# One table of steps for all engines, from batch 1 on, in an attention and Mish kernel

## The chip, the cores and the metric

The kernel runs on one core of one Trainium2 chip. The metric is the device time of one execution in microseconds, as the median of the runs shown; lower is better.

## The reference

Eight batches, each with 8 heads of 512 tokens and 32 states of width 64. First, tokens read from states and states read from tokens, by a softmax each; then both kinds of rows (544 per batch, 512 wide) go through two dense layers with a Mish-like function between them.

```python
scores = scale * (x @ state.T)
xread = softmax(scores) @ state
sread = softmax(scores.T) @ x
rows = concatenate([xread, sread])
h = rows @ w_in
out = (h * tanh(softplus(h))) @ w_out
```

Everything is float32. The kernel reaches that accuracy by splitting each operand into a high part and a low part (in the code h and l: gh and gl, ah and al, swh and swl), and by three matmuls for each product: high by high, low by high, high by low.

## The kernel before

The token rows of a batch never stand in memory as such. For each batch the kernel folds the states into the first weights (`sw_slice`, L567: the state weights, in PSUM as swp, split into swh and swl), so that the first products are the attention weights (aT, split into ah and al) times the state weights. The state reads (`sread`, L495, kept in srds) are collected over all batches and go through the layers once, as an item of their own called "s" between batch 6 and batch 7.

A batch has 8 slots of 2 x 128 hidden columns each. In a slot TensorE makes the first products of both column blocks (`gemm1`, L614, into the banks ph), and ScalarE applies Mish. From batch 2 on the result is held as units: a unit is one half p of a batch's tokens in one slot, so 16 per batch, in ten buffers. `prepare` (L1051) splits a unit into gh and gl, and `consume` (L1079) multiplies it by the second weights (wo). The units of slots 0 to 4 (`SEVEN`, L30) go by seven products of 256 columns instead of four of 512: `prepare` makes four sums on GpSimd for it, and `seven_weights` (L891) makes sums of the weights, once per slot index. The units of slots 5 to 7 go directly. The 8 units of one half p form a span with four PSUM banks (one, two, top, end); the sums of the first two are formed behind the fifth unit, and the results are stored behind the last one (`result`, L675). Batch 1 still uses the direct way for all (`gemm2`, L698), two slots behind.

Beside this, each batch prepares the attention of the next: x is turned (`x_transposed`), moved between partitions by DMA (`x_moved`, L294), multiplied by the states (`scores`), and goes through both softmaxes; `e2_turned` (L389) turns the exps of the second one and moves them by 16 DMAs, and `sread` uses them. The state weights of batches from 2 on come from a copy of w_in in DRAM, 1 MB at a time (`load_w_in_again`, L561).

What sets the order: the steps up to batch 0 are a list written out by hand, in which TensorE, GpSimd, VectorE and ScalarE keep to the program's order (class `InOrder`, L60). At L881 that is switched off for VectorE and ScalarE. From there `around` (L928) and `after` (L960) say per slot what is emitted, and the scheduler orders VectorE, ScalarE and the DMA queue of SP by its own estimate, bound only by the marks of `behind` (L257). `two_next` (L1111) prepares two units at the end of a slot. TensorE and GpSimd keep the order of the program. Batch 6 ends with `sreads_moved` (L536, 16 DMAs, its turned copy in the buffer "wt" that also holds a span's sums) and `sreads_split` (L547). `gemm1_s` (L645) is the first layer of the item "s".

```python
    dve.on = act.on = False
...
        if key == B - 2 and j == 6:
            with behind("mish"):
                sreads_moved()
...
        if j == SEVEN - 1:
            e = spans[key, p]["sums"] = pool.tile([P, 4, 256], F32, tag="wt", name=f"sums_{key}_{p}", bufs=1)
```

Of the kernel before, what the change touches and what calls it, by code (L numbers as in the profile page):

```python
# [9 lines left out]
F32 = mybir.dt.float32  # L10
# [19 lines left out]
SEVEN = 5  # L30
G = 4 * P
# [49 lines left out]
def state_attention_mish_kernel(ctx, tc, x, state, w_in, w_out, out):  # L81
# [454 lines left out]
    def sreads_moved():  # L536

        u = pool.tile([P, 4, B - 1, NS], F32, tag="wt", name="sr_turned", bufs=1)
        dve.transpose(
            u.rearrange("p s b n -> p b s n"), srds[0][:, :B - 1].rearrange("p b k (i d) -> p b (k i) d", i=2))  # L540
        srds["moved"] = pool.tile([P, NC, B - 1, NS], F32, tag="sc", name="sr_moved", bufs=1)
        for s in range(4):
            for c in range(NC):
                nc.sync.dma_start(  # L544
                    srds["moved"][quad(s), c].rearrange("p b n -> p (b n)"), u[quad(c), s].rearrange("p b n -> p (b n)"))

    def sreads_split():  # L547
        both = pool.tile([P, NC, 2, B * NS], F32R, tag="raw", name="srT", bufs=2)
        srT.extend(both[:, :, i] for i in range(2))
        srT.append(both)  # L550
        srT_parts(early, srds["moved"].rearrange("p c b n -> p c (b n)"))

    def sread_transposed():
        pt = first_bank("srTp")[:, :P]
        pe.transpose(pt, srds[0][:, B - 1].rearrange("p k d -> p (k d)"), ident)
        srT_parts(range(B - 1, B), pt.rearrange("p (c n) -> p c n", n=NS))
# [88 lines left out]
    def gemm1_s(j, r, w_rows, unit):  # L645

        for k in range(2):
            fc = 2 * r + k
            ph = (first_bank, misc)[k](f"ph_s_{j}_{r}_{k}")
            w = w_rows[:, :, fc * P:(fc + 1) * P]  # L650
            hi, lo = (pool.tile([P, NC, P], F32R, tag="t", name=f"w{n}_{j}_{r}_{k}", bufs=5) for n in "hl")
            act.copy(hi, w)
            dve.tensor_sub(lo, w, as_f32(hi))

            for c in range(NC):
                pe.matmul(
                    ph, hi[:, c], srT[2][:, c].rearrange("p i t -> p (i t)"), start=(c == 0), stop=(c == NC - 1))
            for c in range(NC):
                pe.matmul(
                    ph[:, :256], lo[:, c], srT[0][:, c], start=False, stop=(c == NC - 1), skip_group_check=True)  # L660
            to = unit[:, 1 - k].rearrange("f h t -> f (h t)")
            act.copy(to, ph[:, 256:])
            dve.tensor_add(to, to, ph[:, :256])
            last["mish"] = act.activation(to, to, AF.Mish)

    def store(key, t, o):
        if key == "s":
            for b4 in range(4):
                r0 = (4 * t + b4) * T + S
                nc.sync.dma_start(out[r0:r0 + NS, :], o[b4 * NS:(b4 + 1) * NS, :])  # L670
        else:
            to = out[key * T:key * T + S, :]
            last["store"] = nc.sync.dma_start(to.rearrange("(p t) e -> p t e", t=NT)[:, t], o)

    def result(key, t, acc, sums=None, op=None):  # L675
        if (key, t) == (B - 1, NT - 1):
            last_o = pool.tile([P, DM], F32, tag="e2T", name=f"o_{key}_{t}", bufs=1)
            for i, part in enumerate((slice(0, 256), slice(256, 512))):
                o = last_o[:, part]
                dve.tensor_tensor(o, acc[:, part], sums[:, i], op)  # L680
                (nc.scalar if part.start else nc.sync).dma_start(
                    out[key * T:key * T + S, part].rearrange("(p t) e -> p t e", t=NT)[:, t, :], o)
            return
        o = pool.tile([P, DM], F32, tag="o", name=f"o_{key}_{t}", bufs=2)
        if sums is not None:
            dve.tensor_tensor(*(a.rearrange("t (h e) -> t h e", h=2) for a in (o, acc)), sums, op)
        elif t % 2 == 0:
            dve.tensor_copy(o, acc)
        else:
            act.copy(o, acc)  # L690
        store(key, t, o)
# [6 lines left out]
    def gemm2(key, fcs, gh, gl, ntok, ts=None):  # L698
# [3 lines left out]
        for t in ts or range(ntok):  # L702
# [9 lines left out]
            if fcs[-1] == NFC - 1:  # L712
                result(key, t, accs[key][t])
# [167 lines left out]
    dve.on = act.on = False  # L881

    with behind("load"):
        sn_next = load_state(2)

# [5 lines left out]
    def seven_weights(j):  # L891
# [5 lines left out]
        pool_e.tensor_add(  # L897
# [5 lines left out]
        low, high = (wo[j][:, 0, n, 256:] for n in range(2))  # L903
        act.copy(high, w[:, 0])
        dve.tensor_sub(low, w[:, 0], as_f32(high))
        low, high = (wx[0][:, j, n] for n in range(2))
        act.copy(high, w[:, 1:])
        dve.tensor_sub(low, w[:, 1:], as_f32(high))

    def products(j):  # L910
# [4 lines left out]
        if j < SEVEN:  # L915
# [9 lines left out]
    own = at1  # L925
    spans = {}

    def around(key, j):  # L928


        nonlocal own, prev, sn_next
        more = key + 1 < B
        if j == 0:
            prev = own
            if more:
                own = attention(key + 1, sn_next, x_ins.pop(key + 1))
                aTs[key + 1] = own["aT"]

        beside = []
        if key == 1 and j == 1:  # L940
            beside += [sw_slice(key, 2)]
# [234 lines left out]
```

## Time and profile before

| what | value |
|---|---|
| median of 3 runs | 667.32 us (666.57 to 667.61) |
| profiled execution | 668.79 us, its span 667.0 us |
| mean granted TensorE clock | 0.976 |
| busy: TensorE, VectorE, ScalarE, GpSimd | 637.2, 427.0, 331.2, 165.3 us |
| matmuls | 5108 |

The span runs from the first to the last instruction of the profiled execution. A busy TensorE is not one at its peak: matmuls are pipelined, and the time of one in the tables includes its way through the array. Waits are put down to what ended them.

### The profile page before, as it was taken

The page shows a single profiled execution, that of the slowest core. Times are in us where ns is not written, and L with a number is a line of the kernel's source. Part 1 is how long each engine was busy: PE and PEld are TensorE (multiplying, and loading weights), DVE is VectorE, ACT ScalarE, POOL GpSimd, SP SyncE. Part 2 cuts the span into 40 slices and gives each one's busy share as a digit, 9 for nine tenths or more (in the row PEclk, how much of TensorE's full clock was granted, in tenths as well). Part 3 has the DMA queues.
Part 4 walks back from the last instruction along what each step waited for, and adds up shares of the span by engine and source line. Part 5 has one row for each costly group of instructions (what it writes and reads, how often), then busy time and mean ns, then how long its engine had stood idle before and what let it go on. Part 6 is the DMA issues. An engine that isn't in the chain of part 4 may idle for free.

```text
span 667.0 us, 12927 instructions
## 1 busy us (share of the span) xinstructions
PE 637.2 (96%) x5108; PEld 533.4 (80%) x5108; DVE 427.0 (64%) x731; ACT 331.2 (50%) x654; POOL 165.3 (25%) x226
## 2 busy tenths in 40 slices
PE   8999999997996979999999999999999799999997
PEld 6776778784885769798988898888887589888996
DVE  6998974777328553877378646964594577335353
ACT  5998852543336433745365434734282375434330
POOL 0000030365223110352017300640050052515200
PEclk9999999998996979999999999999999799999999
DMA  8999826412515252633354254425253341301000
GB/s 331 408 337 315 287 73 173 128 32 64 166 62 186 71 163 66 202 116 110 120 194 124 69 162 148 160 73 158 75 172 96 130 159 28 132 1 28 6 32 32
DMA packets 69036, 89.84 MB, mean 135 GB/s; under 512 B 13808, under 2 KB 42224, under 8 KB 68976
## 3 DMA queue, kind: packets, MB, share of 16 engines
q1 hardware_dynamic: 68544, 88.83, 41.4%
q8 instruction: 40, 0.66, 0.4%
q10 hardware_dynamic: 432, 0.20, 0.1%
q14 instruction: 20, 0.16, 0.1%
HBM read 63.90 MB, written 13.11 MB: 115 GB/s over the span
## 4 chain that ended last, share of the span: by engine, by line
PE 75%; DMA 8%; DVE 6%; SPq 3%; POOL 3%; ACT 2%; issue 1%; DVEq 0%; ACTq 0%
PE ph L73 22%; PE acc_top L73 13%; PE acc_end L73 10%; PE acc L73 6%; PE acc_two L73 6%; PE acc_one L73 6%; PE swp L73 4%; DMA wir<-in_moe_w_in_dram 3%; PE ph_s L73 3%; POOL w_sums L73 3%; DMA x<-in_x_dram 2%; DMA wor<-in_moe_w_out_dram 2%; SPq L544 1%; DVE gl L73 1%; PE acc_s_top L73 1%
## 5 line engine op out<-in xcount | busy, mean ns | idle before, releaser
L73 POOL TENSOR_TENSOR sums<-u 128x256 f32<-128x256 f32 x60 | 53.6, 893 | 310.8 <-DVE u L73 81.0
L73 ACT ACTIVATE u<-ph 128x256 f32<-128x256 f32 x192 | 63.0, 384 | 121.6 <-PE ph L73 119.6
L73 DVE TENSOR_TENSOR gl<-u,gh 128x384 fp32r<-128x384 f32 (+1 forms) x96 | 62.7, 653 | 62.6 <-ACT gh L73 59.6
L73 PE MATMUL ph<-ah,swh 128*128 128x512 f32 (+1 forms) x260 | 83.3, 402 | 10.2 <-DVE swl L73 8.7
L73 PE MATMUL acc_top<-wo,gh 128*128 128x256 f32 (+1 forms) x384 | 92.7, 330 | 0.0
L73 PE MATMUL ph<-al,swh 128*128 128x512 f32 (+1 forms) x260 | 81.5, 396 | 0.2 <-DVE al L73 0.2
L73 PE MATMUL ph<-ah,swl 128*128 128x512 f32 (+1 forms) x260 | 81.4, 394 | 0.1
L73 PE MATMUL acc<-wo,gh 128*128 128x512 f32 x256 | 79.9, 393 | 0.0
L73 POOL TENSOR_TENSOR sums<-sums,u 128x128 f32<-128x128 f32 x120 | 70.3, 586 | 9.4
L73 PEld LDWEIGHTS acc_top<-wo,gh 128*128 128x128 f32 x384 | 64.7, 194 | 8.8 <-DVE srds L73 1.6
L73 ACT CAST gh<-u 128x384 fp32r<-128x384 f32 x60 | 30.9, 515 | 70.2 <-PE acc_end L73 61.3
L73 PEld LDWEIGHTS ph<-ah,swh 128*128 128x128 f32 x260 | 47.7, 194 | 22.3 <-DVE swl L73 9.6
L73 PE MATMUL acc_top<-wo,gl 128*128 128x256 f32 (+1 forms) x192 | 62.7, 326 | 0.0
L73 PEld LDWEIGHTS ph<-al,swh 128*128 128x128 f32 x260 | 49.9, 193 | 11.3 <-DVE al L73 0.4
L73 PEld LDWEIGHTS ph<-ah,swl 128*128 128x128 f32 x260 | 49.7, 192 | 11.4 <-DVE swl L73 0.5
L73 PEld LDWEIGHTS acc<-wo,gh 128*128 128x128 f32 x256 | 47.4, 188 | 12.7 <-issue 2.5
L73 DVE TENSOR_TENSOR gl<-sums,gh 128x512 fp32r<-128x512 f32 x60 | 48.4, 807 | 4.8 <-ACT gh L73 4.7
L73 PE MATMUL acc<-wo,gl 128*128 128x512 f32 x128 | 49.9, 390 | 0.0
L73 DVE TENSOR_TENSOR swl<-swp,swh 128x512 fp32r<-128x512 f32 (+1 forms) x72 | 41.5, 621 | 12.0 <-ACT swh L73 11.8
L73 DVE CAST gh<-u 128x512 fp32r<-128x512 f32 x36 | 16.8, 466 | 49.1 <-PE acc_end L73 39.2
L73 ACT ACT_TABLE_LOAD x35 | 44.9, 1283 | 1.9 <-DVE nm L73 1.3
L73 POOL TENSOR_TENSOR w_sums<-wo 128x1024 f32<-128x1024 f32 x5 | 13.8, 2759 | 126.2 <-DVE wo L73 92.3
(173 smaller groups left out, 1284.3 us busy)
## 6 DMA issues: line engine op xcount, KB each, us to landing
w_in<-w_in_again SPq DMA_DIRECT2D x28, 1024.0 KB, 6.5
x<-in_x_dram SPq DMA_DIRECT2D x32, 256.0 KB, 6.6
wir<-in_moe_w_in_dram SPq DMA_DIRECT2D x16, 512.0 KB, 9.8
wor<-in_moe_w_out_dram SPq DMA_DIRECT2D x16, 512.0 KB, 9.2
out_dram<-o SPq DMA_DIRECT2D x31, 256.0 KB, 2.5
x_rows<-x_turned SPq DMA_DIRECT2D x56, 128.0 KB, 2.4
x_in<-in_x_dram SPq DMA_DIRECT2D x24, 256.0 KB, 4.0
w_in_again<-w_in_sb SPq DMA_DIRECT2D x4, 1024.0 KB, 9.7
```

The source lines that it names most:

```text
L73: made = method(*args, **kwargs)
L544: nc.sync.dma_start(srds["moved"][quad(s), c].rearrange("p b n -> p (b n)"), u[quad(c), s].rearrange("p b n -> p (b n)"))
```

## The change

The line that switches the order off is removed: VectorE and ScalarE keep to the program's order to the end. `around`, `after`, `two_next` and `halves` are replaced by a table with one line per slot. A step that is a generator is named once for each of its pieces (S4 three times: matmuls, copies to high parts, subtractions to low parts). The letters: G0 G1 first products, M0 M1 Mish, P begins a unit (only if fewer than three are ready) and p ends all begun ones, A and B are the half slots in which units are used, X and XD turn and move x, ST the states, SC scores, MM EE second softmax, TU its turning, TR EX NO PR first softmax, sr reads of the states, S and N state weights of this and the next batch, T sums of the weights, w loads of w_in, lx and li loads of x, h and l the parts of batch 1. The DMA queue of SP has no table. In batches 3 to 5 the lines "steady" hold (batch 3 has two of its own); slots of batch 1 are not shown here but for the last.

```diff
+FIRST = 3
...
-    dve.on = act.on = False
...
+        1: """
...
+            G0 M0 G1 M1 h PR0 PR1 A N0 N2 PR0 PR1 N0 N0 N2 N2 B l T1 T1 li""",
+        2: """
+            G0 M0 G1 M1 X0 X1 T2 A X2 X3 XD T2
+            G0 M0 G1 M1 B ST w4 A T2
+            G0 M0 G1 M1 SC sr0 sr1 S4 SC sr0 sr1 S4 S4 w5 lx B P MM0 MM1 p P p
+            P G0 M0 p G1 M1 P p TR0 TR1 A P TR0 TR1 p B
+            P G0 M0 p G1 M1 P p A EE0 EE1 EX0 EX1 P EE0 EE1 w2 p B NO
+            P G0 M0 p G1 M1 P p S6 A P NO S6 S6 w3 p B
+            P G0 M0 p G1 M1 P p PR0 PR1 TU T3 A P p B T3
+            P G0 M0 p T3 G1 M1 P p PR0 PR1 P A P N0 N2 PR0 PR1 N0 N0 N2 N2 p li B""",
...
+        "steady": """
+            P G0 M0 p G1 M1 P p X0 X1 A P X2 X3 XD p B
+            P G0 M0 p G1 M1 P p ST A P p w4 B
+            P G0 M0 p G1 M1 P p A P SC sr0 sr1 S4 SC sr0 sr1 S4 S4 p w5 lx B MM0 MM1
+            P G0 M0 p G1 M1 P p TR0 TR1 A P TR0 TR1 p B
+            P G0 M0 p G1 M1 P p EE0 EE1 EX0 EX1 A EE0 EE1 P w2 p B NO
+            P G0 M0 p G1 M1 P p NO A P S6 S6 S6 w3 p B
+            P G0 M0 p G1 M1 P p PR0 PR1 TU A P p B
+            P G0 M0 p G1 M1 P p PR0 PR1 P A P N0 N2 PR0 PR1 N0 N0 N2 N2 p li B""",
+        B - 2: """
...
+            P G0 M0 p G1 M1 rm P p EE0 EE1 EX0 EX1 A EE0 EE1 P rm w2 p B NO
+            P G0 M0 p G1 M1 P p NO A TU P S6 S6 S6 w3 p B
+            P G0 M0 p G1 M1 P p PR0 PR1 A P p B
+            P G0 M0 p G1 M1 P p PR0 PR1 A P SR0 SR1 N0 N2 SR0 SR1 rs PR0 PR1 N0 N0 N2 N2 rt p W0 W1 B""",
```

In batch 7 a slot is "P G0 M0 p G1 M1 P p A P p B", with S4 and S6 in slots 2 and 3. The first span of batch 2 takes only three units by seven products (`FIRST`). No unit is used in the slot that makes it:

```diff
+    def half_slot(key, j, at):
+        if pending:
+            second((2, 3) if at else (0, 1), not at)
+        elif ready and (ready[0][:2] != (key, 0) or ready[0][2] < j + (j == SLOTS - 1 and at)):
+            consume()
```

The sums of a span are formed in front of its last unit (in the last span behind the fifth one), and the results are added in place and stored from there; the buffers "o" hold the sums of the units instead:

```diff
+        if j == max(n7, SLOTS - 1 if (key, p) != (B - 1, 1) else 0):
+            sums_of(key, p, banks)
...
+            dve.tensor_tensor(sums[:, h], acc[:, h], sums[:, h], op)
...
+            sums = pool.tile([P, 4, P], F32, tag="o", name=f"sums_{key}_{p}_{j}", bufs=2)
```

The moves of the state reads (rm, in slot 4 of batch 6) come in two halves from unit buffers into "wt"; their parts (rs) lie in the buffer of x; the transpose of the last reads (rt) uses a bank of `misc`, as N0 does. The item "s" uses the loads w2 and w3 of batch 7's state weights instead of loads of its own, and its items run one ahead (W0 W1, then in a loop). In `seven_weights` the first of five operations goes from GpSimd to VectorE:

```diff
+        srds["moved"] = pool.tile([P, NC, B - 1, NS], F32, tag="wt", name="sr_moved", bufs=1)
+        for k in range(2):
+            u = pool.tile([P, 2, B - 1, NS], F32, tag="unit", name=f"sr_turned_{k}", bufs=UNITS)
...
-        both = pool.tile([P, NC, 2, B * NS], F32R, tag="raw", name="srT", bufs=2)
+        both = pool.tile([P, NC, 2, B * NS], F32R, tag="x", name="srT", bufs=1)
...
-        pt = first_bank("srTp")[:, :P]
+        pt = misc("srTp")[:, :P]
...
-        pool_e.tensor_add(
+        dve.tensor_add(
```

## Rows read from the trace of the kernel before

**Rows 1.** The page, parts 1 and 2: busy time, and tenths in 40 slices.
```profile
PE 637.2 (96%) x5108; PEld 533.4 (80%) x5108; DVE 427.0 (64%) x731; ACT 331.2 (50%) x654; POOL 165.3 (25%) x226
...
PE   8999999997996979999999999999999799999997
...
PEclk9999999998996979999999999999999799999999
```

**Rows 2.** Busy time by stretches: length, engines (instructions), granted clock, DMA share, GB/s.
```profile
core 0: us, PE busy (x) PEld busy (x) DVE busy (x) ACT busy (x) POOL busy (x), PEclk, DMA share, GB/s
158.79:168.51 9.72, 4.84 (x13) 3.71 (x13) 7.44 (x13) 3.84 (x8) 2.67 (x4) 0.65 0.16 55
198.30:217.25 18.95, 11.94 (x53) 9.54 (x45) 14.76 (x29) 12.29 (x21) 6.71 (x11) 0.73 0.57 188
233.78:245.71 11.93, 8.07 (x33) 6.37 (x25) 7.89 (x13) 2.69 (x8) 2.76 (x4) 0.71 0.53 143
516.03:527.68 11.65, 5.94 (x43) 4.01 (x44) 7.54 (x14) 4.44 (x9) 0.00 (x0) 0.71 0.56 187
337.66:407.68 70.02, 70.02 (x606) 60.31 (x610) 47.39 (x85) 34.66 (x75) 21.18 (x30) 1.00 0.43 131
```

**Rows 3.** The chain that ended last, in batch 3: start, length, what.
```profile
267.68 1.03 PE srp L73 x64
268.71 1.02 PE swp L73 x32
...
272.69 2.72 PE ph L73 x12
...
287.30 0.72 PE acc_one L73 x6
```

**Rows 4.** TensorE in order of time, its waits: start, length, instruction, [idle before <-releaser].
```profile
163.82 1.22 PE L73 MATMUL ph<-ah,swh 128*128 128x512 f32 x2 [4.88 <-DVE swl L73]
...
207.48 0.79 PE L73 MATMUL acc_one<-wx,gh 128*128 128x256 f32 x2 [4.73 <-ACT gh L73]
209.83 0.58 PE L73 MATMUL acc_one<-wx,gl 128*128 128x256 f32 x1 [1.55 <-DVE gl L73]
...
237.70 1.22 PE L73 MATMUL ph<-ah,swh 128*128 128x512 f32 x2 [3.86 <-DVE swl L73]
...
521.74 1.95 PE L73 MATMUL swp<-w_in,bd 64*32 64x256 f32 x30 [6.12 <-DVE srds L73]
```

**Rows 5.** Groups by form: output<-inputs, shapes, count | busy us, mean ns | idle before.
```profile
L73 DVE TENSOR_TENSOR gl<-sums,gh 128x512 fp32r<-128x512 f32 x60 | 48.4, 807 | 4.8 <-ACT gh L73 4.7
...
L73 DVE TENSOR_TENSOR gl<-u,gh 128x384 fp32r<-128x384 f32 x60 | 37.1, 618 | 60.3 <-ACT gh L73 59.6
...
L73 DVE TENSOR_TENSOR swl<-swp,swh 128x512 fp32r<-128x512 f32 x56 | 35.5, 679 | 12.0 <-ACT swh L73 11.8
...
L73 ACT CAST swh<-swp 128x512 fp32r<-128x512 f32 x56 | 29.8, 600 | 18.2 <-PE swp L73 17.9 <-PE ph L73 0.2
...
L73 DVE TENSOR_TENSOR al<-at,ah 128x512 fp32r<-128x512 f32 x16 | 13.2, 858 | 11.1 <-ACT ah L73 11.1
...
L73 DVE TENSOR_TENSOR sums<-acc_two,sums 128x512 f32<-128x512 f32 x12 | 8.3, 688 | 0.8
...
L73 DVE TENSOR_TENSOR o<-acc_top,sums 128x512 f32<-128x512 f32 x12 | 8.2, 682 | 9.6 <-PE acc_top L73 9.6
...
L73 DVE TENSOR_TENSOR sums<-sums,acc_one 128x256 f32<-128x256 f32 x12 | 5.0, 419 | 19.8 <-ACT sums L73 19.8
...
L73 DVE TENSOR_TENSOR sums<-sums,acc_two 128x256 f32<-128x256 f32 x12 | 5.0, 413 | 0.0
```

**Rows 6.** Who waited for whom: us in total, times, longest.
```profile
ACT sums L73 <- DMA sr_moved<-sr_turned: 6.1, 1, 6.1
```

**Rows 7.** SP's queue in order of time: start, length, line, DMA, count.
```profile
168.78 5.19 SPq L304 DMA_DIRECT2D x_rows<-x_turned  x8
...
505.70 11.49 SPq L544 DMA_DIRECT2D sr_moved<-sr_turned  x16
```

**Rows 8.** The page, part 6: DMA issues, KB each, median us from issue to landing.
```profile
w_in<-w_in_again SPq DMA_DIRECT2D x28, 1024.0 KB, 6.5
```

**Rows 9.** The tile w_in: DMA from issue to landing.
```profile
DMA to landing us min/median/max: 5.5/6.5/9.1
```

**Rows 10.** VectorE and GpSimd in order of time, in batch 4.
```profile
343.02 0.56 DVE L73 TENSOR_TENSOR gl<-u,gh 128x384 fp32r<-128x384 f32 x1
...
350.38 1.09 DVE L73 TENSOR_TENSOR gl<-u,gh 128x384 fp32r<-128x384 f32 x1
...
349.87 1.18 POOL L73 TENSOR_TENSOR sums<-u 128x256 f32<-128x256 f32 x1
```

## Blind prediction

> **What bounds the kernel now.** I read the page first. TensorE (PE) is busy 96% of the span, but its row over the 40 slices dips at slices 9 to 14 and 30 to 32, and its granted clock dips in the same slices [rows 1]. So I asked for the busy time by stretches. A whole batch in the middle (337.66 to 407.68) has TensorE busy in all of its 70.02 us, at a clock of 1.00 [rows 2]; the chain of waits there is matmul behind matmul [rows 3]. Nothing that reorders VectorE, ScalarE or the queues can shorten those batches: only TensorE's own work could, and the change keeps it, but for two units priced below. What can go is in four stretches of the same table, where the granted clock averages 0.65 to 0.73 [rows 2]. TensorE's order of time shows the wait in each: 4.88 us for the low halves of the next batch's state weights (swl), 4.73 us (and 1.55 us two matmuls later) for the parts of a unit (gh, gl), 3.86 us for swl again, and 6.12 us behind the state reads (srds) [rows 4].
>
> **What each stretch costs.** The chain gives the unit prices: 12 matmuls of 512 columns take 2.72 us, 6 of 256 columns 0.72 us (so 21, a unit by seven products, 2.52 us), 64 state reads 1.03 us, 32 state-weight matmuls 1.02 us [rows 3]. From the ends of the stretches: 158.79 to 168.51 holds 12 matmuls, 9.72 - 2.72 = 7.0 us lost. 198.30 to 217.25 holds two slots of first products and one unit, 18.95 - 2 x 2.72 - 2.52 = 11.0. 233.78 to 245.71 holds 24 wide matmuls, 11.93 - 5.44 = 6.5. 516.03 to 527.68 holds 12 that should have followed the state weights at once, 11.65 - 2.72 = 8.9. Sum 33.4 us. Of these some 2 to 3 us each are not waiting but the slow clock after it (7.0 - 4.88 = 2.1; 6.5 - 3.86 = 2.6; 8.9 - 6.12 = 2.8): the matmuls then run at 1.2 instead of 2.4 GHz for a while.
>
> **The change, part by part.**
> *The first three stretches.* They come from the scheduler's placing of VectorE and ScalarE work. In the table, slot 7 of batches 1 and 2 puts the state weights (N0 N2), their copies and low halves ahead of the half slot B, and leaves the weight sums T behind it. Worked out for batch 1 from the first G: TensorE needs 2.72 (G) + 2.72 (A) + 2 x 1.02 (N0 N2) + 2.72 (B) = 10.2 us until the next batch's G0. N0's matmuls end at 6.5; two ScalarE copies at about 0.55 and two VectorE subtractions at about 0.6, one behind the other (their mean single durations, 0.60 and 0.68, overlap a little) [rows 5], end at 8.4. So swl is there 1.8 us early: 7.0 and 6.5 us go. The 11.0 us go because the first span of batch 2 now starts a slot later (half slots at 2.0 to 2.2 drain batch 1), takes three units by seven products instead of five, and no unit may be used in the slot that makes it: a unit is begun two half slots ahead of its use. The two direct units add 2 x (2.72 - 2.52) = 0.4 us.
> *The state reads of batch 6.* Before, the turned reads lie in the buffer that the span's sums need, and ScalarE waits 6.1 us for their 16 moves [rows 6]; these moves take 11.49 us of SP's queue [rows 7]. Now they lie in unit buffers, start in slot 4 instead of behind slot 6, and the weights of the state rows are those that batch 7 uses anyway, which takes four loads of 1 MB off the queue. The 8.9 us go, but slot 7 of batch 6 gets a wait that I can see in the table: the transpose of the last state read (rt) stands on TensorE ahead of B, in a bank that N0 uses, so it waits for N0's first subtraction. On VectorE that one stands behind two scalings of the reads, the subtraction of srT (after a 0.95 us copy) and two of al. Counted from the reads' first matmul: srT is done at 3.2, al at 4.4, N0's first at 5.1, while TensorE is through N2 at 3.1: 2.0 us idle. What the clock does after 2.0 us idle no row shows: between 0 and the 2.8 us above; nearest are the waits of 3.86 us and more, which are longer, so I take 1.0. The reads also need the moves of e2T, 16 issues behind the 16 of the state reads: 0 to 3 us late, I take 0.7. Then two low halves are late by 0.3 each. Sum 4.3.
> *Loads a slot earlier.* The state weights S4 now come in slot 2. In batch 2 the 8 moves of x take 5.2 us of SP [rows 7], end some 12.8 us after G0, and only then is the buffer of the 1 MB load free, which lands 6.5 us later (5.5 to 9.1) [rows 8, 9]: at 18.3 to 21.9, where TensorE arrives at 18.4. I take 0.8 us, bounds 0 and 3.5. In later batches slots 0 and 1 are 4.4 us longer, so it is covered by about 1 us.
> *The sums of a span moved to its last unit.* Four operations (one on ScalarE, three on VectorE) and the two results now stand together at slots 3 and 7, ahead of the next span's first unit, which needs the four banks back. On VectorE that is 0.42 + 0.69 + 0.41 + 0.68 + 0.68 = 2.9 us of mean durations [rows 5]. Slot 7 is the tight one: VectorE can start on it at 3.6 (after G1's activations) with a direct unit (about 1.1), al (1.3), four swl (2.6), two units' low halves (2 x 1.3) and then these 2.9: with the mean durations it ends at some 14 to 15, and TensorE, which starts the next span at 12.9 and meets the banks in the order one, two, top, end every 0.72 us, is held up by 0 to 1.4 us. I take 0.7 at each of four such places (batches 2 to 5), 2.8; slot 3 has over 1 us to spare, and batch 7 has no attention.
> *VectorE beside GpSimd.* The durations used here are means over both cases, and the cases differ: one low half of 384 elements took 0.56 us with GpSimd still and 1.09 us while GpSimd summed [rows 10]. The Trainium skill ("SBUF — State Buffer", section "SBUF: two separate sides") speaks against packing them together: it calls their shared port an exclusive lock, the loser blocked for the whole instruction. The trace shows less: 0.53 us was added beside a GpSimd operation of 1.18 us. By that rule each hold-up of slot 7 would be 1.2 us instead of 0.7, and the sum 2 us more.
> *The rest.* The first operation of the weight sums goes from GpSimd to VectorE, off TensorE's path, since the unit that needs it comes a slot or more later. Exps stand together, so fewer table loads; ScalarE waits anyway. Startup is the same code, but SP's order is still the scheduler's; 0 to 5 us for that and for what I overlooked, I take 1.0.
>
> **The sum.** -33.4 + 0.4 + 4.3 + 0.8 + 2.8 + 1.0 = -24.1 us. The profiled execution took 668.79 us around its span of 667.0; it would come to 644.7. The median of the runs is 667.32, 1.5 us below, and the forecast is made against it: 643.2 us.
>
> **The rivals.**
> *Waits change place (22%).* The order is right but the loads are late: S4 in batches 3 to 6, covered by 1 us, late by 1.6 each if the load takes its longest 9.1 instead of 6.5 [rows 9] (6.4 us), 2.7 more in batch 2, 2.3 more at the reads in batch 6 and 1 us more of slow clock. 643.2 + 12.4 = about 656 us. For it: SP's queue is not in the table. Against: that queue stands still for most of a batch (the 5.2 and 11.5 us are its longest runs).
> *Handing over a span becomes the bound (10%), the slower side.* There are 12 places where one span's banks go to the next. If VectorE comes to the sums only when TensorE has left the last unit, all 2.9 us are exposed at each: 34.8 us instead of 2.8, so 643.2 + 32.0 = 675 us. It decides from the point where VectorE is over 3 us later at the end of a slot than I work out. For it: the order is now fixed, and every wait at the head of VectorE holds what stands behind it. Against: VectorE is busy 47.4 of 70.0 us in a batch [rows 2], and only slot 7 has more work than time.
> *The change does not do what it says (4%).* The stalls hang on data that no order brings sooner; then 667.3 + 0.4 = 667.7 us.
>
> **The numbers.** My forecast keeps 64%: 643.2 us, between 635.5 (all four stretches gone, only rt left: 667.3 - 33.4 + 0.4 + 2.0 = 636.3, and 1 us from the startup) and 652. The range reaches into the first rival to 657. A measurement of this kernel can tell about 0.2% (1.3 us) from no change. Faster takes the forecast and the first rival, 0.86; slower the second, with a little of the third, 0.11; the rest 0.03.
>
> **What would show it.** Right: TensorE's row without dips in slices 9 to 14; the three waits of 3.9 to 4.9 us gone; the middle batches 70 to 71 us long; in batch 6's slot 7 one wait of 2 to 3 us at the transpose of the last read; sr_moved nowhere among ScalarE's waits. First rival: matmuls of swp behind w_in loads, or the reads behind e2T. Second: the first matmuls of a unit waiting for sums or o on VectorE, a dozen times. Wrong altogether: a middle batch longer than 73 us.

## The result, and the profile of the changed kernel

The changed kernel takes 651.46 us (median of 4 runs, 650.42 to 652.56) beside 667.47 us for the kernel before on the same chip: a ratio of 0.9755, 95% interval 0.9723 to 0.9786, so 16.0 us faster. The profiled execution took 652.01 us around a span of 650.2 us, 16.8 us less than the span before. The forecast was 643.2 us: the sign and most of the mechanism held, and some 8 us of the gain did not come.

The page, parts 1 and 2, of the changed kernel (compare [rows 1]):

```profile
PE 631.5 (97%) x5090; PEld 526.6 (81%) x5090; DVE 429.7 (66%) x737; ACT 311.2 (48%) x638; POOL 136.0 (21%) x215
...
PE   8999999999989989999999999999999899999997
...
PEclk9999999999979999999999999999999999999999
```

TensorE's row had a 7, a 6, a 7 and a 7 between its ends; now it has three 8s. The granted clock was below 9 tenths in four slices and is so in one. TensorE's waits in order of time tell what it waits for now (start, length, instruction, idle before and releaser; only the instructions that waited, from 84 us on; two further waits like the one at 304.80 are left out):

```profile
118.46 1.05 PE L74 MATMUL srp<-x_again,e2T 128*32 128x64 f32 x58 [1.33 <-DMA e2T<-u]
181.90 1.96 PE L74 MATMUL swp<-w_in,bd 64*32 64x256 f32 x32 [4.36 <-DMA w_in<-w_in_again]
223.64 1.64 PE L74 MATMUL swp<-w_in,bd 64*32 64x256 f32 x32 [0.88 <-ACT u L74]
229.53 0.73 PE L74 MATMUL ph<-ah,swh 128*128 128x512 f32 x2 [0.97 <-DVE swl L74]
233.15 0.51 PE L74 MATMUL acc_one<-wo,gh 128*128 128x256 f32 x2 [0.60 <-DVE sums L74]
234.33 0.51 PE L74 MATMUL acc_two<-wx,gh 128*128 128x256 f32 x2 [0.20 <-DVE sums L74]
304.80 0.50 PE L74 MATMUL acc_two<-wx,gh 128*128 128x256 f32 x2 [0.16 <-DVE sums L74]
510.70 1.22 PE L74 MATMUL swp<-w_in,bd 64*32 64x256 f32 x32 [0.94 <-DMA w_in<-w_in_again]
512.72 0.33 PE L74 MATMUL srTp<-ident,srds 128*128 128x128 f32 x1 [0.81 <-DVE swl L74]
```

The waits of [rows 4] are gone but for one: there is no 4.88 us for swl in batch 1, no 4.73 us for gh, no 6.12 us behind srds, and 0.97 us are left for swl where 3.86 stood. In their place stands one large wait that the prediction had priced at 0.8 us, for the 1 MB load of S4 in batch 2, and a group of small ones in slot 7 of batch 2, to which the 0.97 us belong. The windows of the changed kernel (columns as in [rows 2]: batch 2 around S4, its slot 7, a whole batch in the middle, slot 7 of batch 6):

```profile
174.90:190.00 15.10, 10.74 (x151) 7.37 (x150) 4.88 (x10) 3.91 (x9) 0.00 (x0) 0.77 0.94 313
216.10:235.00 18.90, 16.18 (x124) 11.15 (x123) 15.14 (x23) 9.69 (x23) 11.12 (x16) 1.00 0.28 85
323.42:393.87 70.45, 70.30 (x607) 60.33 (x610) 45.98 (x85) 31.82 (x73) 18.14 (x30) 1.00 0.43 130
502.10:515.64 13.54, 11.79 (x166) 8.90 (x165) 7.47 (x14) 8.38 (x18) 0.00 (x0) 1.00 0.31 93
```

From these, with the unit prices of [rows 3], the lost time of each place: **S4 in batch 2.** The state reads end at 177.5, the next slot starts at 188.22; between them lie 32 state-weight matmuls and 12 wide ones, 3.74 us of work in 10.7 us: 7.0 lost, 4.4 of them waiting and 2.6 at the slow clock. **Slot 7 of batch 2.** From 216.13 (its first matmul) to 233.15 there are 4 x 2.72 + 2.04 = 12.9 us of work: 4.1 lost, and 0.4 more at acc_two. **Batch 6, slot 7.** 13.54 us hold some 11.3 us of work: 2.2 lost. **Middle batches.** 70.45 us instead of 70.02, 1.3 us over three batches. **Reads of batch 1.** 1.3 us.

### The profile page after: what moved, and what is told of

It is laid out like the page before. It is cut to its first block, busy times and chain, and to the rows that moved or that the text cites. A ratio compares the mean times of both kernels' runs of the same rounds, so it can differ in the third digit from the quotient of the medians.

```text
span 650.2 us, 12856 instructions
## 1 busy us (share of the span) xinstructions
PE 631.5 (97%) x5090; PEld 526.6 (81%) x5090; DVE 429.7 (66%) x737; ACT 311.2 (48%) x638; POOL 136.0 (21%) x215
## 4 chain that ended last, share of the span: by engine, by line
PE 81%; DVE 9%; DMA 4%; SPq 3%; ACT 2%; issue 1%; POOL 0%; DVEq 0%; ACTq 0%
PE ph L74 23%; PE acc_top L74 12%; PE acc L74 11%; PE acc_end L74 9%; PE acc_two L74 6%; PE acc_one L74 6%; PE swp L74 4%; PE ph_s L74 3%; SPq L402 3%; DVE gl L74 2%; DMA wir<-in_moe_w_in_dram 2%; DVE swl L74 2%; DVE sums L74 1%; PE acc_s_top L74 1%; PE srp L74 1%; PE sc L74 1%
## 5 line engine op out<-in xcount | busy, mean ns | idle before, releaser
L74 POOL TENSOR_TENSOR sums<-u 128x256 f32<-128x256 f32 x58 | 45.8, 789 | 267.8 <-DVE gl L74 266.7
L74 PE MATMUL ph<-ah,swh 128*128 128x512 f32 (+1 forms) x260 | 80.4, 391 | 1.8 <-DVE swl L74 1.0
L74 PE MATMUL ph<-al,swh 128*128 128x512 f32 (+1 forms) x260 | 79.6, 388 | 0.2 <-DVE al L74 0.2
L74 PE MATMUL ph<-ah,swl 128*128 128x512 f32 (+1 forms) x260 | 79.6, 388 | 0.0
L74 DVE TENSOR_TENSOR gl<-u,gh 128x384 fp32r<-128x384 f32 (+1 forms) x96 | 60.3, 629 | 13.3 <-ACT gh L74 9.1
L74 POOL TENSOR_TENSOR sums<-sums,u 128x128 f32<-128x128 f32 x116 | 63.5, 547 | 9.1
L74 PEld LDWEIGHTS ph<-al,swh 128*128 128x128 f32 x260 | 48.5, 188 | 10.7 <-DVE al L74 0.4
L74 PEld LDWEIGHTS ph<-ah,swh 128*128 128x128 f32 x260 | 46.7, 188 | 12.8 <-ACT g L74 1.7
L74 POOL TENSOR_TENSOR w_sums<-w_sums 128x256 f32<-128x256 f32 x20 | 16.6, 830 | 189.5 <-DVE w_sums L74 188.3
L74 DVE TENSOR_TENSOR gl<-sums,gh 128x512 fp32r<-128x512 f32 x58 | 43.1, 743 | 17.5 <-ACT gh L74 17.5
L74 ACT CAST swh<-swp 128x512 fp32r<-128x512 f32 (+1 forms) x72 | 34.7, 549 | 35.3 <-PE swp L74 35.2
L74 ACT CAST gh<-u 128x384 fp32r<-128x384 f32 x58 | 29.4, 515 | 43.5 <-PE acc_end L74 22.8
```

Source lines behind the costliest of these rows:

```text
L74: made = method(*args, **kwargs)
```

## The experiments

Each ratio is to the kernel before on the same chip, with its 95% interval. The runs come from several chips, on which the median of the kernel before lay between 667.1 and 669.0 us, so a difference between the times of two runs is good to some 1 us; where the ratios say something else, both are given.

### The load of S4, one slot later

```diff
 2:
-            G0 M0 G1 M1 SC sr0 sr1 S4 SC sr0 sr1 S4 S4 w5 lx B P MM0 MM1 p P p
-            P G0 M0 p G1 M1 P p TR0 TR1 A P TR0 TR1 p B
+            G0 M0 G1 M1 SC sr0 sr1 SC sr0 sr1 w5 lx B P MM0 MM1 p P p
+            P G0 M0 p G1 M1 P p TR0 TR1 S4 A P TR0 TR1 S4 S4 p B
```

> The state weights S4 of batch 2 are made one slot later (slot 3 instead of slot 2); their 1 MB load, the moves of x in front of it and all else stay. Theory (the load is late): in the changed kernel TensorE stands 4.36 us idle at 181.90 for this load and then runs at the slow clock, 7.1 us lost between 176 and 197. A slot later the load has long landed, so nearly all of it goes: 651.5 - 6.8 = about 644.7 us, ratio to the kernel before 0.966, and no wait on w_in in batch 2. Rival (the stall only changes place): the low halves of S4 then come late for the first products of slot 4, or the next 1 MB load is pushed back, and a wait of 3 us or more stands in slot 3 or 4 instead: 649 to 651.5 us, ratio 0.973 to 0.976.

Measured: 648.42 us, ratio 0.9700 (0.9681 to 0.9719). The time lies between the two and nearer the rival: the wait for the load is gone altogether, but only 3.0 of 6.8 us came (3.7 by the ratios). The rival's wait of 3 us or more is not there either; two smaller ones are. TensorE's order of time in this run, and VectorE's between two of its lines:

```profile
184.81 1.10 PE L74 MATMUL swp<-w_in,bd 64*32 64x256 f32 x32 [0.85 <-ACT u L74]
...
193.23 1.10 PE L74 MATMUL ph<-ah,swl 128*128 128x512 f32 x2 [1.17 <-DVE swl L74]
```

```profile
187.53 1.30 DVE L74 STREAM_TRANSPOSE e<-scs 128x512 f32<-128x512 f32 x2
...
191.89 0.69 DVE L74 TENSOR_TENSOR e<-e,mx 128x512 f32<-128x512 f32 x1
192.50 1.28 DVE L74 TENSOR_TENSOR swl<-swp,swh 128x512 fp32r<-128x512 f32 x2
```

So the late load was what TensorE waited for, as the theory has it. But a step put elsewhere in a fixed order takes a new place in three queues: S4 now wanted a bank that Mish had not yet left, and its low halves stood behind the first softmax's operations on VectorE, though its copies were done at 188.4.

### The weight sums T3, earlier; and its first operation back on GpSimd

In the changed kernel the chain that ended last runs, in slot 7 of batch 2, through VectorE, GpSimd and ScalarE (start, length, what):

```profile
217.74 1.12 DVE w_sums L74
...
218.92 0.75 POOL w_sums L74
...
221.43 0.74 POOL w_sums L74
...
222.19 0.84 ACT wx L74
```

ScalarE reaches the copy of these sums 2.10 us before they are there, and slot 7's Mish (u, which the wait at 223.64 names) is next in its order.

```diff
-            P G0 M0 p G1 M1 P p PR0 PR1 TU T3 A P p B T3
-            P G0 M0 p T3 G1 M1 P p PR0 PR1 P A P N0 N2 PR0 PR1 N0 N0 N2 N2 p li B
+            P T3 G0 M0 p G1 M1 P p PR0 PR1 TU A T3 P p B T3
+            P G0 M0 p G1 M1 P p PR0 PR1 P A P N0 N2 PR0 PR1 N0 N0 N2 N2 p li B
```

> The three pieces of the weight sums T3 stand half a slot to a slot earlier in batch 2 (start, middle and end of slot 6 instead of middle and end of slot 6 and start of slot 7). Theory (the weight sums): slot 7 of batch 2 loses 4.4 us because ScalarE's copy of these sums waits 2.1 us for four GpSimd operations (3.24 us), and Mish, the bank for N2 and the low halves stand behind it in the fixed order. Then some 3.4 of the 4.4 us go: about 648 us, ratio 0.971, and the 0.88 us at N2 (released by ScalarE) and the 0.97 us at the next first products (released by swl) are gone. Rival (the hand-over of the span, as the prediction priced it): the sums and results at the end of slot 7 fill VectorE whatever stands before; the waits for swl and sums stay, at most 1 us is saved: 650.5 to 651.5 us, ratio 0.975.

Measured: 648.24 us, ratio 0.9699 (0.9680 to 0.9718): the theory. Between 200 and 235 us one wait of 0.16 us for sums is left; those for u and swl are gone, so they were only what the late sums of the weights left behind them. Then the first operation alone went back:

```diff
-        dve.tensor_add(
+        pool_e.tensor_add(
             w.rearrange("p (k e) c -> p k (e c)", k=2), as_f32(wo[j][:, :, 0]), as_f32(wo[j][:, :, 1]))
```

> The changed kernel with the first operation of the weight sums back on GpSimd, where the kernel before had it (there 2.76 us on GpSimd, 1.18 us on VectorE now). Theory (the weight sums of T3 are a chain that ends at the Mish of slot 7 in batch 2): 1.6 us later there, and as much in T4's copies in batch 3 if these have no slack: 1.6 to 3.2 us slower than the changed kernel, 653.1 to 654.7 us, ratio 0.978 to 0.980; TensorE's wait for u at N2 of batch 2 grows from 0.88 to 2 us or more. Rival (the prediction's: this step is off TensorE's path): within 0.6 us of the changed kernel, 651 to 652 us, ratio 0.9745 to 0.976.

Measured: 652.04 us (648.94 to 653.81), ratio 0.9767 (0.9739 to 0.9794), which can't be told from the changed kernel. The median is the rival's (0.04 us beyond it); the trace is neither's. GpSimd's order of time shows T3's sums more than 20 us earlier, since on GpSimd nothing stands in front of them:

```profile
195.53 2.41 POOL L74 TENSOR_TENSOR w_sums<-wo 128x1024 f32<-128x1024 f32 x1
198.01 3.93 POOL L74 TENSOR_TENSOR w_sums<-w_sums 128x256 f32<-128x256 f32 x4
```

In slot 7 of batch 2 no wait over 0.2 us is left. Part of what that gave was lost again: the exps of batch 1 went to their queue at 152.75 instead of 150.14, mostly since one of VectorE's operations took 2.83 us beside GpSimd's sum (shown in the last section), and S4's wait grew from 4.36 to 5.09 us, with 1.1 us more at the scores in front of it; the wait at the reads of batch 1 was 2.00 instead of 1.33. The traced execution, 649.83 us, is still 2.2 us under that of the changed kernel; the five runs lie 4.9 us apart, so their median decides nothing here. So for T3 alone:

```diff
-        dve.tensor_add(
+        (pool_e if j == 3 else dve).tensor_add(
```

> The changed kernel with the first operation of the weight sums on GpSimd for T3 alone. Theory, formed on the run with all of them on GpSimd (there GpSimd made T3's sums at 195.5 us, 22 us before VectorE reaches them in the changed kernel, and slot 7 of batch 2 lost 0.6 instead of 4.4 us, while batch 1 lost some 3 us more): putting this operation into VectorE's fixed order is what made the loss of slot 7, so T3 alone gives some 3.5 us and costs nothing in batch 1: 648 us, ratio 0.971, as in the run with T3 earlier. Rival (the loss of slot 7 hangs on how late batch 1 was in that run, which gave VectorE time): the loss of 4.4 us stays, 651 to 652.5 us, ratio 0.975 to 0.977.

Measured: 649.27 us (647.75 to 651.01), ratio 0.9718 (0.9694 to 0.9742), the theory's side; no wait over 0.2 us in slot 7 of batch 2, and S4's wait 4.21 us, as without the edit. Only 2.2 us are seen in the time (2.5 by the ratios; the reads of batch 1 waited 1.70 instead of 1.33 us), but the loss of slot 7 was made by putting this one operation into VectorE's fixed order.

### The sums of a span behind the fifth unit again

```diff
-        if j == max(n7, SLOTS - 1 if (key, p) != (B - 1, 1) else 0):
+        late = (key, p) in ((2, 0), (B - 2, 0))
+        if j == max(n7, SLOTS - 1 if late else 0):
```

> The sums of a span are formed behind its fifth unit again, as in the kernel before, in all spans but the first ones of batches 2 and 6 (where the buffer is in use). Theory of the prediction (each hand-over at slot 7 of batches 3 to 5 holds TensorE up by 0.7 us): three such places and a few smaller ones, 2.1 us or more gained: 649.4 us, ratio 0.972. Rival (VectorE has the time, only the waits of 0.15 us at the first matmul after a hand-over are real): 0.1 to 0.3 us per place, at most 0.8 us in all: 650.7 to 651.5 us, ratio 0.974 to 0.976; batches 3 to 5 stay at 70.2 to 70.5 us.

Measured: 651.54 us, ratio 0.9747 (0.9728 to 0.9766): no difference in time. But the batches are shorter: the state reads start at 254.09, 324.14, 394.19 and 464.23, so 70.05 us apart instead of 70.45. The late sums cost 0.4 us a batch, 1.2 in all, between the two theories; in this run batch 1 was 1.2 us later (S4 waited 4.81 us) and hid it.

### The fixed order off

```diff
+    dve.on = act.on = False
     A12, A22, A11, A21 = range(4)
```

> VectorE and ScalarE are let off the program's order from batch 1 on, as in the kernel before; the table, the units, the buffers stay. Theory (the fixed order of the two engines makes the gain in batches 1 and 2): the scheduler places VectorE's and ScalarE's work by its own estimate again, and waits of 3 to 5 us for swl, gh or gl come back at several places: 661 to 672 us, ratio 0.99 to 1.007. Rival (the gain comes from what the table gives TensorE and from the units being begun two half slots ahead, the order of the other two engines hardly matters): 650 to 655 us, ratio 0.974 to 0.981.

Measured: 665.31 us, ratio 0.9961 (0.9940 to 0.9982): the theory's time, 13.9 us of the 16. Its waits of 3 to 5 us are not there; there are more, and smaller ones, the longest 2.14 us. VectorE's order of time in batch 1's slot 7, and TensorE's, show what the scheduler does there:

```profile
163.27 1.29 DVE L74 TENSOR_TENSOR swl<-swp,swh 128x512 fp32r<-128x512 f32 x2 [1.94 <-ACT swh L74]
165.33 0.71 DVE L74 STREAM_TRANSPOSE x_turned<-x_in 128x512 f32<-128x512 f32 x1 [0.77 <-DMA x_in<-in_x_dram]
167.06 0.71 DVE L74 STREAM_TRANSPOSE x_turned<-x_in 128x512 f32<-128x512 f32 x1 [1.02 <-DMA x_in<-in_x_dram]
167.69 1.25 DVE L74 TENSOR_TENSOR swl<-swp,swh 128x512 fp32r<-128x512 f32 x2
```

```profile
168.49 0.73 PE L74 MATMUL ph<-ah,swh 128*128 128x512 f32 x2 [2.14 <-DVE swl L74]
```

Two transposes of x, whose load is still on its way, stand ahead of the low halves that TensorE waits for. Two transposes stand ahead of the low halves in slot 7 of each later batch too (batches 2 to 5: waits for swl of 2.02, 2.08, 1.10 and 1.23 us; the kernel before had none in batches 3 to 5). Before its slot 7, in batch 1, TensorE waits 1.82 us at the reads of batch 0, 1.49 us for sm on VectorE and 2.09 us for g on ScalarE; S4 of batch 2, on the other hand, waits for no load there. The 4.73 us for gh, however, did not come back: between 198 and 217 us TensorE waits for nothing. So the order of these two engines is not what removed that stretch. The later start of batch 2's first span and its three units by seven products are what is left of the prediction's account; no run undid them, so this part is not shown.

With ScalarE alone let off:

```diff
+    act.on = False
     A12, A22, A11, A21 = range(4)
```

> Only ScalarE is let off the program's order from batch 1 on, VectorE keeps it. With both off 665.3 us were measured, with both on 651.5 us. Theory (VectorE's order is what counts: the scheduler put transposes of x, which wait for their load, ahead of the low halves): without ScalarE's order most of the gain stays, 651 to 655 us, ratio 0.974 to 0.980. Rival (either engine alone undoes it, since the scheduler's placing of ScalarE's copies holds the low halves as well): 658 to 666 us, ratio 0.985 to 0.997.

Measured: 653.90 us, ratio 0.9808 (0.9791 to 0.9825): the theory. With VectorE's order kept, 11.4 of the 13.9 us stay (10.2 of 13.8 by the ratios).

### The state reads: the place or the buffer

Two runs. The first takes the old buffers and the old place (there with one rm, since all 16 moves are one piece), the second the old place alone:

```diff
-        srds["moved"] = pool.tile([P, NC, B - 1, NS], F32, tag="wt", name="sr_moved", bufs=1)
...
-            u = pool.tile([P, 2, B - 1, NS], F32, tag="unit", name=f"sr_turned_{k}", bufs=UNITS)
...
+        u = pool.tile([P, 4, B - 1, NS], F32, tag="wt", name="sr_turned", bufs=1)
...
+        srds["moved"] = pool.tile([P, NC, B - 1, NS], F32, tag="sc", name="sr_moved", bufs=1)
```

```diff
-            P G0 M0 p G1 M1 rm P p EE0 EE1 EX0 EX1 A EE0 EE1 P rm w2 p B NO
+            P G0 M0 p G1 M1 P p EE0 EE1 EX0 EX1 A EE0 EE1 P w2 p B NO
...
-            P G0 M0 p G1 M1 P p PR0 PR1 A P p B
+            P G0 M0 p G1 M1 P p PR0 PR1 A P p B rm rm
```

> The state reads of batch 6 are turned and moved as in the kernel before: turned copy in the buffer of the span's sums, moved copy in the buffer of the scores, all of it behind slot 6; the rest is the changed kernel. Theory (the start time is what counts): in the changed kernel the 16 moves run from 483.3 to 494.4 us and are ready when batch 6 reaches slot 7; from behind slot 6 they run from about 502 to 514, their split waits for them some 6 us longer on ScalarE, and al and swl stand behind it on VectorE, so slot 7 loses 6 to 9 us more: 657.5 to 660.5 us, ratio 0.984 to 0.989. Rival (nothing waits for these reads until the item of the state rows begins): at most 2 us lost: 651.5 to 653.5 us, ratio 0.975 to 0.978.

> Only the place is undone: the state reads are turned and moved behind slot 6 of batch 6, in the changed kernel's buffers. Theory (the start time is what counts): the same moves at the same late time, so within 1.5 us of the run with the old buffers: 657.5 to 660.5 us, ratio 0.984 to 0.989. Rival (the buffer is what counts: with the old one the sums of the span wait for the moves, with the new one nothing does): 651.5 to 653.5 us here, ratio 0.975 to 0.978, and 6 us or more above that with the old buffers.

Measured: 661.48 us, ratio 0.9894 (0.9876 to 0.9912), and 661.36 us, ratio 0.9888 (0.9872 to 0.9904): 10 us slower than the changed kernel, alike, and 1 us above what the theory allowed. It is the place. TensorE's order of time with the old buffers, then with the new ones:

```profile
520.12 0.48 PE L74 MATMUL srTp<-ident,srds 128*128 128x128 f32 x1 [9.66 <-DVE swl L74]
```

```profile
511.20 2.56 PE L74 MATMUL srp<-x,e2T 128*32 128x64 f32 x64 [4.06 <-ACT u L74]
...
520.65 0.45 PE L74 MATMUL srTp<-ident,srds 128*128 128x128 f32 x1 [3.29 <-DVE swl L74]
```

With the new buffers the wait comes in two parts: Mish needs unit buffers that the moves still read (ScalarE waited 7.2 us for sr_moved), then the split of the reads waits 3.6 us more.

### The losses together

```diff
 1:
-            G0 M0 G1 M1 h S2 S2 S2 B l tu ST w1
+            G0 M0 G1 M1 tu h S2 S2 S2 B l ST w1
 2:
+            G0 M0 G1 M1 SC sr0 sr1 SC sr0 sr1 w5 lx B P MM0 MM1 p P p
+            P G0 M0 p S4 G1 M1 P p S4 TR0 TR1 A S4 P TR0 TR1 p B
 B - 2:
-            P G0 M0 p G1 M1 P p NO A TU P S6 S6 S6 w3 p B
+            P G0 M0 p G1 M1 P p NO A P S6 S6 S6 w3 TU p B
...
-            if key > 1 and i == 4 and key < B - 1:
+            if key > 2 and i == 4 and key < B - 1:
```

and T3 earlier as above (the two lines of batch 2 stand for those of the first run).

> Four moves in the table together: S4 of batch 2 between the two first products of slot 3, in two banks that slot leaves free, with its copies and low halves ahead of the first softmax's; T3 as in the run with T3 earlier; the turning of the exps (tu) of batch 1 at the start of its slot instead of the end; in batch 6 the last load of state weights (w3) ahead of the turning of its exps. Theory (the losses are these four, and they add up): S4 7.1 us to under 1, T3's 3.2 us, 1.3 us at the reads of batch 1 and 0.9 us at N2 of batch 6, some 11 us of 651.5: about 640.5 us, ratio 0.959. Rival (S4 still finds its load or VectorE late, as in the run where it stood one slot later and kept 3.1 us of the 7.1; the two small ones are hidden elsewhere): 643.5 to 646 us, ratio 0.963 to 0.968.

Measured: 642.68 us, ratio 0.9604 (0.9589 to 0.9619), between the two: by the ratio nearer the theory, by the time nearer the rival. S4 and slot 7 of batch 2 have no wait over 0.2 us left; the reads of batch 1 still wait 0.65 us; and in batch 6 the wait only moved: N2 has its load in time, and the transpose of the last read waits 2.07 instead of 0.81 us. Hence the next run:

```diff
-            P G0 M0 p G1 M1 P p PR0 PR1 A P SR0 SR1 N0 N2 SR0 SR1 rs PR0 PR1 N0 N0 N2 N2 rt p W0 W1 B
+            P G0 M0 p G1 M1 P p PR0 PR1 A P PR0 PR1 SR0 SR1 N0 N2 SR0 SR1 rs N0 N0 N2 N2 rt p W0 W1 B
```

> The four moves together, and one more: in slot 7 of batch 6 the two subtractions of al stand ahead of the state reads instead of behind them. Theory (the prediction's account of rt: the transpose of the last read waits for N0's first low half, and that stands on VectorE behind the scaled reads, srT and two of al): with al (1.28 us) done while VectorE is idle before the reads, the wait of 2.07 us at this transpose, seen with the four moves, falls to 0.8 us: 641.4 us, ratio 0.9585. Rival (another of the things in front sets it, ScalarE's copies or the moves of the reads): the wait stays above 1.6 us and the time at 642.7 us, ratio 0.9604.

Measured: 640.46 us, ratio 0.9602 (0.9584 to 0.9620): the time lies beyond the theory, the ratio beside that of the run before it, so the times alone don't decide. The wait does: 2.07 us became 0.90.

```profile
501.51 0.33 PE L74 MATMUL srTp<-ident,srds 128*128 128x128 f32 x1 [0.90 <-DVE swl L74]
```

Last, the edit of the early sums added to this one:

> The five moves in the table, and the sums of a span behind its fifth unit in all spans but two. Theory (the late sums cost 0.4 us per batch, as the lengths of batches 3 to 5 showed: 70.45 us with the sums late, 70.05 us with them early; in the run with the early sums alone batch 1 was 1.2 us later and hid it): batches 3 to 5 are 70.05 us long and the time is 1.2 us under that of the five moves alone, 640.46 us: 639.2 us, ratio 0.9582. Rival (what is won there is lost again in slot 7 of batch 6, whose wait for swl grows, as it did with the early sums alone): 640.5 us, ratio 0.960, with a wait of 1.5 us or more at the transpose of the last read.

Measured: 638.99 us (637.72 to 639.35), ratio 0.9552 (0.9532 to 0.9572): the theory, and 12.5 us faster than the changed kernel (13.5 by the ratios). The page's rows have no dip left, and the state reads of batches 3, 4 and 5 (TensorE's order of time) stand 70.04 and 70.05 us apart:

```profile
PE   8999999999999999999999999999999999999997
...
PEclk9999999999999999999999999999999999999999
```

```profile
312.73 1.10 PE L74 MATMUL srp<-x,e2T 128*32 128x64 f32 x64
...
382.77 1.10 PE L74 MATMUL srp<-x,e2T 128*32 128x64 f32 x64
...
452.82 1.10 PE L74 MATMUL srp<-x,e2T 128*32 128x64 f32 x64
```

## Why the prediction was right, and where it was 8 us off

| term | forecast, us | measured, us |
|---|---|---|
| four stretches | -33.4 | -33.4, taken over: their waits are gone, the 0.97 us left is counted in slot 7 of batch 2 |
| two direct units | +0.4 | +0.4 (by price; not seen apart) |
| batch 6, slot 7 | +4.3 | +2.2 |
| S4 in batch 2 | +0.8 | +7.0 |
| hand-over, batches 3 to 5 | +2.1 | +1.3 |
| slot 7 of batch 2 (0.7 there as a hand-over) | +0.7 | +4.5 |
| rest | +1.0 | +1.3 (the reads of batch 1) |
| sum | -24.1 | -16.7, beside 16.8 in the span |

The sign was right, and the sum fits, but the time lies only 0.5 us inside the upper end of the forecast's range (652) and nearer the first rival's 656 than the forecast's 643.2. Part of that is luck: S4 and slot 7 of batch 2 cost 10.0 us more than forecast, batch 6 and the hand-over 2.9 us less. Nor is the table as exact as its last line looks: a wait of 0.55 us that the kernel before had at 88.45, at the reads of batch 0, is gone as well and stands in no row.

*The four stretches* were read rightly as time that TensorE lost waiting and not working. That the first three came "from the scheduler's placing" is shown in part. With the order off most of the gain went, but not in the old way: the low halves waited 2.14 and 2.02 us at the ends of batches 1 and 2 instead of 4.88 and 3.86, and the rest stands in batch 1 and in batches 3 to 5. The 11.0 us around gh did not come back with the order off; that they hang on the units, as the prediction also said, is argued and not shown. For the state reads the prediction named both buffer and place; the runs show that the place alone carries it, some 10 us.

*S4 in batch 2* is the term that was mis-sized: 7.0 instead of 0.8, above its upper bound of 3.5. The prediction let the moves of x end 12.8 us after G0 and the load land 6.5 us behind them, at 19.3. In the changed kernel G0 is at 159.0, TensorE is there at 18.5 us after it, as worked out, and the load lands at 22.8. SP's queue shows why:

```profile
150.14 10.86 SPq L402 DMA_DIRECT2D e2T<-u  x16
161.10 2.07 SPq L136 DMA_DIRECT2D x_in<-in_x_dram  x4
167.79 5.21 SPq L305 DMA_DIRECT2D x_rows<-x_turned  x8
173.10 1.55 SPq L219 DMA_DIRECT2D sn<-in_state_dram  x3
174.93 0.59 SPq L568 DMA_DIRECT2D w_in<-w_in_again  x1
```

x itself comes late, since its load stands behind the 16 moves of e2T of the slot before: the moves of x end at 14.0 instead of 12.8. Then loads of the states go first, 1.9 us until the load of S4 starts, and it takes 6.8 us. Together 3.5 us that the prediction left out by looking at the moves of x alone and not at what is in front of and behind them; and the clock, which it left out here, took 2.6 us more. The run with S4 a slot later shows that it is this load. That the 16 moves set its time fits the run with all first operations on GpSimd: there they began 2.6 us later, and the load of x, the moves of x, the load of S4 and its matmuls all came 2.6 to 2.9 us later.

*Slot 7 of batch 2* failed at the sentence that the first operation of the weight sums lies "off TensorE's path, since the unit that needs it comes a slot or more later". The unit did come later. But the wait was not the unit's: ScalarE's copy waited for GpSimd, GpSimd for VectorE's operation at its fixed place, and Mish stood behind the copy. The prediction asked who needs the result, and not who stands behind the one that waits for it.

*The hand-over* cost 0.4 us a batch instead of 0.7. The mechanism (waits for sums at the first matmuls of the next span) is there. VectorE was not through sooner than forecast: in slot 7 of batch 3 it ended the second result 15.2 us after the slot's first product (290.73 to 305.94; the last section has the line), where the prediction had 14 to 15. But it gives the banks back one by one. Bank one was ready at 303.56, before TensorE came to it at 303.76; bank two at 304.74, which cost 0.16 us of waiting; top at 305.34 and end at 305.94, before their turns at 305.61 and 306.32. By the rule of the Trainium skill ("SBUF — State Buffer", section "SBUF: two separate sides"), as the prediction applied it, 1.2 us each were to be expected, and the runs show 0.4. The rival that it becomes the bound (675 us) is out; so is the one that the change does nothing.

*VectorE beside GpSimd.* The prediction's "the trace shows less" was a misreading of [rows 10]. It set the 0.53 us added against all 1.18 us of the GpSimd operation. But that one had begun at 349.87 and VectorE's at 350.38, so 0.67 us of it were left, and VectorE's ended 0.42 us after it. The last section has a row that shows it without doubt.

*Batch 6, slot 7* was predicted at 2.0 us idle, 1.0 clock, 0.7 for e2T and 0.6 for low halves. In the changed kernel 1.75 us were idle, shared between N2's late load and rt; with the load in time the wait at rt alone was 2.07 us, and putting al ahead took 1.2 us of it away, the chain that the prediction had worked out. The clock cost nothing: behind the 2.07 us the granted clock reads 1.00. e2T was not late.

*The first rival* (loads behind which swp waits) was half right: it named the place, 2.7 us more in batch 2, and its sign, a matmul of swp behind a load of w_in, stands there; but S4 in batches 3 to 6 waited for nothing in the changed kernel, and for 0.3 to 0.7 us in batch 3 of four runs whose batch 2 was shorter.

## What to carry to other kernels

Where engines keep a written order, an operation costs what stands behind it: price a step that waits by the next instruction on the waiting engine, not by who uses its result, and do it for every engine of its chain. For a load that a table moves earlier, follow the transfer queue back to the load before the load: here 1.2 us came from the moves of the slot before, through x, and 1.9 us from loads that stood between. Moving one step by half a slot to a slot gave some 3 us here (S4 later, T3 earlier), but look in the trace for the bank and the queue that it meets at its new place.

## What the runs showed of the hardware that was not expected

VectorE beside GpSimd, in the changed kernel at a hand-over (order of time, VectorE, then GpSimd):

```profile
300.93 0.69 DVE L74 TENSOR_TENSOR gl<-sums,gh 128x512 fp32r<-128x512 f32 x1
...
302.00 1.23 DVE L74 TENSOR_TENSOR gl<-sums,gh 128x512 fp32r<-128x512 f32 x1
...
303.60 0.69 DVE L74 TENSOR_TENSOR sums<-acc_two,sums 128x512 f32<-128x512 f32 x1
...
305.26 0.68 DVE L74 TENSOR_TENSOR sums<-acc_end,sums 128x512 f32<-128x512 f32 x1
```

```profile
301.69 0.98 POOL L74 TENSOR_TENSOR sums<-u 128x256 f32<-128x256 f32 x1 [20.74 <-DVE gl L74]
...
302.76 1.33 POOL L74 TENSOR_TENSOR sums<-sums,u 128x128 f32<-128x128 f32 x2
```

The same low half takes 0.69 us with GpSimd still and 1.23 us beside it, but the sum that reads one operand from PSUM takes 0.69 us beside it too. The Trainium skill ("SBUF — State Buffer", section "SBUF: two separate sides") restricts the lock, against GpSimd, to VectorE operations with two SBUF inputs (and to its fast modes): on the PSUM operand this trace agrees. So the hand-over's own operations on VectorE, which all read PSUM, are not slowed here; the low halves in front of them are.

The 0.54 us added look like less than a block for the length of the GpSimd operation, 0.98 us. But that one had begun 0.31 us earlier, 0.67 us of it were left, and the low half ended 0.56 us after it. The run with all first operations on GpSimd has a longer one, beside a multiplication of the first softmax (VectorE, then GpSimd):

```profile
143.60 0.69 DVE L74 TENSOR_TENSOR e<-e,r 128x512 f32<-128x512 f32 x1
...
146.20 2.83 DVE L74 TENSOR_TENSOR e<-e,r 128x512 f32<-128x512 f32 x1
```

```profile
146.08 2.40 POOL L74 TENSOR_TENSOR w_sums<-wo 128x1024 f32<-128x1024 f32 x1 [46.95 <-DVE wx L74]
```

The same multiplication takes 0.69 us with GpSimd still and 2.83 us when it starts 0.12 us behind the GpSimd operation: it ends 0.55 us after that one. The Trainium skill says in the same section that the one of the two that starts second is fully blocked, since the first holds the port for its whole instruction; this trace agrees. In a trace the blocked row does not start later, it gets longer.

TensorE's clock after a wait. Windows behind the waits of 0.88 and 4.36 us in the changed kernel (columns as in [rows 2]):

```profile
223.64:225.20 1.56, 1.56 (x32) 0.62 (x32) 1.46 (x3) 1.56 (x5) 1.56 (x2) 1.00 0.17 43
181.90:186.00 4.10, 4.10 (x37) 2.54 (x38) 1.29 (x2) 1.08 (x2) 0.00 (x0) 0.50 1.04 389
```

Behind the long one the granted clock is 0.50, 1.2 instead of 2.4 GHz, for these 4.1 us. Behind the short one it reads 1.00, and still 32 matmuls took 1.64 instead of 1.09 us; behind 0.94 us, at 510.70, they took 1.22. The length of a wait alone does not tell what the clock does next: behind the 2.07 us of the run with four moves it read 1.00, behind the 2.14 us of the run with the order off (168.40 to 170.50) 0.65. What makes the difference was not tried.
